# Gram products beside the up and sp products, and off-diagonal products in three pieces, in a fused delta-rule attention and expert-layer kernel

## The chip, the cores and the metric

One core of one Trainium2 chip runs the kernel. Its engines are named as in the profile: PE (TensorE; PEld is its weight load), DVE (VectorE), ACT (ScalarE), POOL (GpSimd) and SP (the queue that issues transfers). The metric is the device time of one execution in microseconds (us); the time of a kernel is the median of its runs.

## The reference

Three stages follow each other, all in float32. For each of 32 (batch, head) pairs a state of 48 by 48 runs through 768 positions:

```python
k_n = k / (np.linalg.norm(k, axis=-1, keepdims=True) + 1e-06)
for t in range(S):
    y[:, :, t] = q_t @ state
    v_old = state.T @ k_t
    state = state + b_t * outer(k_t, v_t - v_old)
```

Its output, as 3072 rows of 384, goes through two expert layers, whose products are the bulk of the arithmetic:

```python
x = (x @ w_a) * (x @ w_b) @ w_out                       # width 1536
h = x @ w_in                                            # width 2048
out = (np.maximum(h, 0) + alpha * np.minimum(h, 0)) @ w_out
```

## The kernel before

**Chunks.** The sequence is cut into NSC = 6 chunks c of 128 positions, and each chunk into two steps j of 64. The recurrence inside a step is solved as a triangular system. The 32 pairs lie as 16 pairs on each of two halves of the 128 partitions (index x), so a product of 48 or 64 rows uses one quarter (a quadrant) of PE's array, and the two halves use two quadrants that share neither rows nor columns.

**Per chunk.** `gram` (L210) computes for four of the 16 pairs the Gram products of the next chunk N: keys with keys and keys with queries, 128 columns wide, in one PSUM bank, and DVE masks them at L222 (keys, into `ef`), L223 and L224 (queries, back into `Z`). Eight such blocks make a chunk's Grams. `fold` (L263) copies a part of `ef` on ACT. `inverting` (L270) then inverts the 32 by 32 diagonal blocks by 30 rounds of two DVE instructions (L293, L294), and `diagonal` (L297) transposes the result into `hw` (L301) and `TT` (L305). `offdiag` (L312) forms the off-diagonal part: for each j first w = ef x hw (L321, copied into `hw` by ACT at L324), then xx = hw x TT (L332, copied into `TT` at L335), all in tiles of 32 by 32. `step` (L339) then runs rp (v minus keys times state, L354, L355), up (L364, copied into `SU`), sp (the next state, L377) and yp (the output, L385, L386), each in two halves of 8 pairs with one bank each.

**Order.** All engines follow the order in which the program is written. The first expert layer of the chunk before is a generator `moe1`: p products (x times w_a or w_b, L578) and o products (L580), one matmul at a time. `run(moe, n, PIECE)` puts n of them between two blocks of the attention, n being FILLS[c] = 10. A counter `now` counts matmuls (plus PIECE for a block); what DVE, ACT and POOL do in the background (weight decoding, the inversion through `leisurely`) is emitted when that counter says that the engine is free. The loop around the change, in c = 1 to 4:

```python
for j in range(2):
    for i, _ in enumerate(A.step(c, j, L)):
        going = run(moe, fill, PIECE) and going
        for _ in range(2):
            if grams:
                A.gram(N, *grams.pop(0), "chain" if c == 1 else "pre")
                going = run(moe, fill, PIECE) and going
```

So two Gram blocks follow each of the first four blocks of step 0. Of PSUM's banks, `chain` has two, `pre` one, `ab` two for the p products, `out` three for o. In c = 1 `pre` belongs to the decoding of weights, and Grams and off-diagonal products use `chain`; later they use `pre`.

**Chunk 0** has no expert products yet. It runs the same functions with `early` in place of `run`, and there the Grams of chunk 1 were made ahead (`gram_keys`, `gram_queries`). Its `offdiag` blocks stand between masks and folds of chunk 1, in the loop over `A.offdiag` with OFF. After chunk 5 the rest of the first and then the second layer run without attention.

Of the kernel before, what the change touches and what calls it, by code (L numbers as in the profile page):

```python
# [31 lines left out]
FILLS = (0, 10, 10, 10, 10, 10)  # L32
# [18 lines left out]
OFF = (6, 6, 10, 10)  # L51
# [29 lines left out]
class Attention:  # L81
# [128 lines left out]
    def gram(s, L, j, i4, tag="pre"):  # L210

        nc = s.nc
        Z, ef = L["Z"][j], L["ef"]
        if j not in L.setdefault("mb", {}):
            s.masks(L, j)
        mb = L["mb"][j]
        g = s.bank("g", tag).rearrange("p (i n) -> p i n", n=128)
        for i in range(4):
            nc.tensor.matmul(g[0:64, i, :], Z[64:112, 0, i4 + i, :], Z[64:112, 0:2, i4 + i, :], start=True, stop=True)  # L219
            nc.tensor.matmul(g[64:128, i, :], Z[0:48, 0, i4 + i, :], Z[0:48, 0:3:2, i4 + i, :], start=True, stop=True)  # L220
        u0 = j * 16 + i4
        nc.vector.tensor_tensor(ef[:, u0 : u0 + 4, :], g[:, :, 0:64], mb[:, i4 : i4 + 4, :], ALU.mult)  # L222
        nc.vector.tensor_tensor(Z[0:64, 1, i4 : i4 + 4, :], g[0:64, :, 64:128], mb[0:64, i4 : i4 + 4, :], ALU.mult)  # L223
        nc.vector.tensor_tensor(Z[64:128, 2, i4 : i4 + 4, :], g[64:128, :, 64:128], mb[64:128, i4 : i4 + 4, :], ALU.mult)  # L224
        s.spend(DVE, 5)

    def gram_keys(s, L, j, i8, tag):

        nc, Z = s.nc, L["Z"][j]
        g = s.bank("g", tag).rearrange("p (i n) -> p i n", n=64)  # L230
        for i in range(8):
            nc.tensor.matmul(g[0:64, i, :], Z[64:112, 0, i8 + i, :], Z[64:112, 0, i8 + i, :], start=True, stop=True)
            nc.tensor.matmul(g[64:128, i, :], Z[0:48, 0, i8 + i, :], Z[0:48, 0, i8 + i, :], start=True, stop=True)
        return g

# [4 lines left out]
    def gram_queries(s, L, j, i8, tag):  # L240

        nc, Z = s.nc, L["Z"][j]
        g = s.bank("gq", tag).rearrange("p (i n) -> p i n", n=64)
        for i in range(8):
            nc.tensor.matmul(g[0:64, i, :], Z[64:112, 0, i8 + i, :], Z[64:112, 1, i8 + i, :], start=True, stop=True)
            nc.tensor.matmul(g[64:128, i, :], Z[0:48, 0, i8 + i, :], Z[0:48, 2, i8 + i, :], start=True, stop=True)
        return g
# [64 lines left out]
    def offdiag(s, L, tags=("pre", "pre")):  # L312
# [3 lines left out]
        for j in range(2):  # L316
            w = s.bank("w", tags[j]).rearrange("p (i n) -> p i n", n=32)
            for i in range(16):
# [3 lines left out]
            for x in range(2):  # L322
                r = slice(64 * x + 32, 64 * x + 64)
                nc.scalar.copy(hw[r, j * 16 : j * 16 + 16, :], w[r])  # L324
                s.spend(ACT, 2.3)
            yield
        for j in range(2):
            xx = s.bank("xx", tags[j]).rearrange("p (i n) -> p i n", n=32)
            for i in range(16):
# [3 lines left out]
            for x in range(2):  # L333
                r = slice(64 * x, 64 * x + 32)
                nc.scalar.copy(TT[r, j * 16 : j * 16 + 16, 32:64], xx[r])  # L335
                s.spend(ACT, 2.3)
            yield

    def step(s, c, j, L):  # L339

        nc, ap = s.nc, s.ap
        st = c * 2 + j
# [5 lines left out]
        for o, hs in halves:  # L348
# [3 lines left out]
            rp = bank("rp")  # L352
            for i in range(8):
                nc.tensor.matmul(rp[0:64, i, :], Z[64:112, 0, o + i, :], SU[0][64:112, o + i, :], start=True, stop=True)  # L354
                nc.tensor.matmul(rp[64:128, i, :], Z[0:48, 0, o + i, :], SU[1][0:48, o + i, :], start=True, stop=True)  # L355
            nc.vector.tensor_tensor(R[:, hs, :], rp, R[:, hs, :], ALU.subtract)
            s.spend(DVE, 2.3)
            yield
        for o, hs in halves:
            up = bank("up")  # L360
            for i in range(8):
                for x in range(2):
                    sl = slice(64 * x, 64 * x + 64)
                    nc.tensor.matmul(up[sl, i, :], s.TT[sl, j, o + i, :], R[sl, o + i, :], start=True, stop=True)  # L364
            for x in range(2):
                sl = slice(64 * x, 64 * x + 64)
                nc.scalar.copy(SU[x][sl, hs, :], up[sl])
                s.spend(ACT, 1.9)
            yield
        for o, hs in halves:  # L370
            if st == 2 * NSC - 1:
                break
            sp = bank("sp")
            for i in range(8):
                for x in range(2):
                    sl = slice(64 * x, 64 * x + 64)
                    nc.tensor.matmul(sp[64 * x : 64 * x + 48, i, :], bk[sl, j, o + i, :], SU[x][sl, o + i, :], start=True, stop=True)  # L377
            nc.vector.tensor_tensor(SN[1][0:48, hs, :], SU[0][64:112, hs, :], sp[0:48], ALU.subtract)
            s.spend(DVE, 4.4)
            nc.vector.tensor_tensor(SN[0][64:112, hs, :], SU[1][0:48, hs, :], sp[64:112], ALU.subtract)  # L380
            yield
# [22 lines left out]
def attn_moe_kernel(tc, kt, qt, kn, vn, beta, w_a, w_b, w_o, w_in, w_o2, alpha, out):  # L404
    nc = tc.nc
    with ExitStack() as ctx:
# [96 lines left out]
        def prepare():  # L503
# [3 lines left out]
            if m is not None:  # L507
                while (m, i) not in decoded or {"u", "g"} & set(under):
# [129 lines left out]
        GRAMS = [(j, i4) for j in range(2) for i4 in range(0, 16, 4)]  # L638
# [42 lines left out]
        def staging():  # L681

            t = None
            for tag, k in STAGES:
                for q in range(k):
                    while under.count(tag) >= RING.get(tag, 1) or tag in closed:
                        yield None
                    under.append(tag)
                    rooms.append(tag)
# [13 lines left out]
        def decode1(depth):  # L703
# [5 lines left out]
            raw = None if W[m][0] is None and m == M1 - 2 and "late" in under else next(words)  # L709
# [84 lines left out]
        for i, _ in enumerate(A.offdiag(L, ("chain", "chain"))):  # L794
            if i in (1, 2):

                for h in range(2):
                    A.mask_keys(N, i - 1, 8 * h, keys.pop(0))
                    spend(DVE, 3)
                A.fold(N, i - 1)  # L800
            if i == 2:
                rooms1.append("pre")
                inv = A.inverting(N, room)
                idle = leisurely(inv)
            early(OFF[i])
        L["y"] = [None, None]
# [25 lines left out]
        for c in range(NSC):  # L832
# [3 lines left out]
            if c > 0:  # L836
                N = A.load(c + 1) if c + 1 < NSC else None
                grams = []
# [14 lines left out]
                for i, _ in enumerate(A.offdiag(L, ("chain", "chain") if c == 1 else ("pre", "pre"))):  # L853
                    going = run(moe, fill, PIECE) and going
                    if N is not None:
                        if i == 1:
                            norms = A.norms(N)
                        if i >= 1:
                            next(norms, None)
                if N is not None:  # L860
                    A.masks(N, 0)
                    grams = list(GRAMS)
                closed.clear()
                L["y"] = [None, None]
                for j in range(2):
                    for i, _ in enumerate(A.step(c, j, L)):
# [4 lines left out]
                        for _ in range(2):  # L871
# [189 lines left out]
```

## Time and profile before

| what | us |
|---|---|
| median of 3 runs | 1169.42 (1168.88 to 1171.29) |
| the profiled execution, its own time | 1172.91 |
| its span, first to last instruction | 1171.2 |
| PE busy | 1085.0 |
| DVE busy | 683.3 |
| POOL busy | 540.9 |
| ACT busy | 463.1 |

The span is that of one profiled execution; 1.7 us lie around it. The busy time of an engine is the union of its instructions' times. A product of two float32 operands shows as two records of PE, so the 16 matmuls of an up block are 32 records. Times in the trace count from the span's start. The five chunks with expert products go from the first w product of one chunk to that of the next.

### The profile page before, as it was taken

The page shows a single profiled execution, that of the slowest core. Times are in us where ns is not written, and L with a number is a line of the kernel's source. Part 1 is how long each engine was busy: PE and PEld are TensorE (multiplying, and loading weights), DVE is VectorE, ACT ScalarE, POOL GpSimd, SP SyncE. Part 2 cuts the span into 40 slices and gives each one's busy share as a digit, 9 for nine tenths or more (in the row PEclk, how much of TensorE's full clock was granted, in tenths as well). Part 3 has the DMA queues.
Part 4 walks back from the last instruction along what each step waited for, and adds up shares of the span by engine and source line. Part 5 has one row for each costly group of instructions (what it writes and reads, how often), then busy time and mean ns, then how long its engine had stood idle before and what let it go on. Part 6 is the DMA issues. An engine that isn't in the chain of part 4 may idle for free.

```text
span 1171.2 us, 22896 instructions
## 1 busy us (share of the span) xinstructions
PE 1085.0 (93%) x9536; PEld 905.4 (77%) x9536; DVE 683.3 (58%) x1141; ACT 463.1 (40%) x895; POOL 540.9 (46%) x459
## 2 busy tenths in 40 slices
PE   5367999699998999999999999999999999999998
PEld 5365677477776777777777887789999999999997
DVE  7887679843894389438927558834343433434332
ACT  4364664353335333533367577622221112112111
POOL 6264686434443444545436668823333333333332
PEclk9577999889999999999999999999999999999999
DMA  9105232300030003000023134010201002020101
GB/s 279 61 30 150 95 110 82 95 29 15 2 96 29 15 2 96 29 15 4 12 69 110 55 104 154 26 55 1 54 1 42 14 1 55 1 55 1 27 1 27
DMA packets 25591, 61.35 MB, mean 52 GB/s; under 512 B 4496, under 2 KB 7568, under 8 KB 25488
## 3 DMA queue, kind: packets, MB, share of 16 engines
q1 hardware_dynamic: 25168, 59.50, 17.2%
q8 instruction: 75, 1.23, 0.4%
q10 hardware_dynamic: 320, 0.39, 0.1%
q14 instruction: 28, 0.23, 0.1%
HBM read 50.44 MB, written 9.44 MB: 51 GB/s over the span
## 4 chain that ended last, share of the span: by engine, by line
PE 57%; DVE 19%; issue 3%; ACT 3%; POOL 1%; DMA 0%; ACTq 0%; DVEq 0%; POOLq 0%
PE h L489 17%; PE o L942 17%; PE p L578 11%; PE o L580 6%; DVE itmp L293 5%; DVE eu L294 5%; PE g L219 2%; DVE a L533 2%; DVE wu L477 1%; DVE v L763 1%; ACT wu L476 1%; PE up L364 1%; PE xx L332 1%; PE rp L354 1%; DVE hw L301 1%
## 5 line engine op out<-in xcount | busy, mean ns | idle before, releaser
L578 PE MATMUL p<-x,wu 128*128 128x512 f32 x1296 | 345.8, 408 | 18.5 <-DVE a L533 9.5
L578 PEld LDWEIGHTS p<-x,wu 128*128 128x128 f32 x1296 | 240.9, 192 | 78.1 <-issue 8.2
L477 POOL TENSOR_TENSOR wu<-W,wu 128x384 fp32r<-128x384 f32 x166 | 175.4, 1060 | 238.0 <-ACT wu L476 208.3
L477 POOL TENSOR_TENSOR g<-neg,g 128x512 fp32r<-128x512 f32 x95 | 123.3, 1298 | 276.7 <-ACT g L476 276.7
L942 PE MATMUL o<-v,g 128*128 128x384 f32 x1152 | 217.8, 337 | 0.2 <-ACT g L476 0.2
L489 PE MATMUL h<-x,v 128*128 128x512 f32 x864 | 215.2, 393 | 0.0
L942 PEld LDWEIGHTS o<-v,g 128*128 128x128 f32 x1152 | 204.7, 188 | 9.1 <-ACT g L476 0.5
L933 DVE TENSOR_SCALAR neg<-h,al 128x512 f32<-128x512 f32 (+1 forms) x97 | 72.3, 746 | 218.2 <-PE h L489 217.3
L476 ACT CAST g<-neg 128x512 fp32r<-128x512 f32 (+1 forms) x97 | 59.7, 615 | 325.5 <-DVE neg L934 311.9
L489 PEld LDWEIGHTS h<-x,v 128*128 128x128 f32 x864 | 160.7, 188 | 29.3
L580 PE MATMUL o<-g,wu 128*128 128x512 f32 x648 | 173.8, 402 | 0.8 <-DVE wu L477 0.5
L580 PEld LDWEIGHTS o<-g,wu 128*128 128x128 f32 x648 | 119.5, 190 | 29.7 <-issue 2.9
L476 ACT CAST wu<-W 128x384 fp32r<-128x384 f32 x216 | 107.7, 510 | 23.8 <-PE o L580 12.4
L542 POOL TENSOR_TENSOR g<-a,g 128x512 fp32r<-128x512 f32 x71 | 94.4, 1329 | 40.0 <-ACT g L537 40.0
L537 ACT CAST g<-a 128x512 fp32r<-128x512 f32 x72 | 44.5, 618 | 126.1 <-DVE a L533 125.8
L533 DVE TENSOR_TENSOR a<-p,a 128x512 f32<-128x512 f32 x72 | 49.5, 687 | 67.1 <-PE p L578 40.6
L477 DVE TENSOR_TENSOR wu<-W,wu 128x384 fp32r<-128x384 f32 x50 | 49.9, 998 | 58.5 <-ACT wu L476 57.2
L293 DVE TENSOR_TENSOR itmp<-eu 128x30 f32<-128x30 f32 (+14 forms) x120 | 68.2, 568 | 3.2
L294 DVE TENSOR_TENSOR eu<-eu,itmp 128x30 f32<-128x30 f32 (+14 forms) x120 | 67.5, 563 | 4.1
L934 DVE SCALAR_TENSOR_TENSOR neg<-h,neg 128x512 f32<-128x512 f32 (+1 forms) x97 | 66.5, 686 | 3.3
L530 ACT COPY a<-p 128x512 f32<-128x512 f32 x72 | 42.0, 584 | 45.8 <-PE p L578 34.0
L321 PE MATMUL w<-hw,ef 32*32 32x32 f32 x768 | 17.3, 207 | 28.7 <-DVE hw L301 24.0
(111 smaller groups left out, 1308.8 us busy)
## 6 DMA issues: line engine op xcount, KB each, us to landing
v<-in_w_in_dram SPq DMA_DIRECT2D x16, 384.0 KB, 3.5
v<-in_w_o_dram SPq DMA_DIRECT2D x16, 384.0 KB, 3.3
k<-in_kn_dram SPq DMA_DIRECT2D x6, 768.0 KB, 6.6
Z<-in_kt_dram SPq DMA_DIRECT2D x24, 192.0 KB, 7.2
Z<-in_qt_dram SPq DMA_DIRECT2D x24, 192.0 KB, 6.6
v<-in_vn_dram SPq DMA_DIRECT2D x12, 384.0 KB, 3.1
raw<-in_w_a_dram SPq DMA_DIRECT2D x12, 384.0 KB, 6.2
raw<-in_w_b_dram SPq DMA_DIRECT2D x12, 384.0 KB, 5.0
```

The costliest lines, as they stand in the source:

```text
L293: nc.vector.tensor_tensor(tm, a, b, ALU.mult)
L294: nc.vector.tensor_tensor(eu[:, m + 1 : 32, 0:m], eu[:, m + 1 : 32, 0:m], tm, ALU.add)
L476: nc.scalar.copy(dst[:, 0], src)
L477: eng.tensor_tensor(dst[:, 1], src, f32(dst[:, 0]), ALU.subtract)
L489: nc.tensor.matmul(p, u[:, a, kk * 128 : kk * 128 + 128], xs[kk][:, b], start=(n == 0), stop=(n == 3 * KT - 1))
L533: nc.vector.tensor_tensor(a[m], ab.pop((m, 1)), a[m], ALU.mult)
L542: (nc.vector if last else nc.gpsimd).tensor_tensor(g[m][:, 1], a[m], f32(g[m][:, 0]), ALU.subtract)
L578: nc.tensor.matmul(ab[m, t], wu, X[c][kk][:, q], start=(n == 0), stop=(n == 8))
L580: nc.tensor.matmul(o[kk], wu, g[m][:, q], start=(m == 0 and n < 3), stop=(m == M1 - 1 and n > 5),)
L933: nc.vector.tensor_scalar(t[:, cs], h[:, cs], 0.0, al[:, m : m + 1], ALU.min, ALU.mult)
L934: nc.vector.scalar_tensor_tensor(t[:, cs], h[:, cs], 0.0, t[:, cs], ALU.max, ALU.add)
L942: nc.tensor.matmul(o[n], g[:, a, n * 128 : n * 128 + 128], V[m][1][:, b], start=(m == 0 and i == 0), stop=(m == M2 - 1 and i == 2),)
```

## The change

1. `gram` goes. Its products are cut into blocks of eight pairs and 64 columns, keys or queries alone (`grams`), and become mates: `mate` hands `step` a function that issues the two Gram products of pair i, and `step` calls it right after the two products of its own pair i. up and sp have mates, in step 0 the four blocks of keys, in step 1 the four of queries. A mate uses the two quadrants that its host doesn't, and a bank of its own: `chain` in c = 1 and `pre` later.
2. `offdiag` makes three pieces of four: w of j=0; xx of j=0 with w of j=1, pair by pair; xx of j=1, which is returned as a function and is the mate of the first rp of step 0, two pairs for one of rp. In chunk 0 the third piece stands by itself.
3. The mask tiles of the two steps get a room each (`mk`, `mb`), and both are made after the second rp. The stages of `norms` move from between the off-diagonal pieces to the first rp blocks.
4. There are fewer stops, so the fill between them is 13 in c = 1 and 14 later, and OFF has three entries. Rooms of staged weights are now told apart by number and not by tag alone.

```diff
-FILLS = (0, 10, 10, 10, 10, 10)
+FILLS = (0, 13, 14, 14, 14, 14)
-OFF = (6, 6, 10, 10)
+OFF = (8, 10, 12)
@@ masks
-            mb = s.ap.tile([128, 16, 64], F32, tag="mb", name="mb", bufs=1)
+            mb = s.ap.tile([128, 16, 64], F32, tag=("mk", "mb")[j], name="mb", bufs=1)
@@ gram goes; new
+    def grams(s, L, j, i8, tag, a, b, go=True):
+        nc, Z = s.nc, L["Z"][j]
+        g = s.bank("g", tag).rearrange("p (i n) -> p i n", n=64)
+        def products(i):
+            nc.tensor.matmul(g[0:64, i, :], Z[64:112, 0, i8 + i, :], Z[64:112, a, i8 + i, :], start=True, stop=True)
+            nc.tensor.matmul(g[64:128, i, :], Z[0:48, 0, i8 + i, :], Z[0:48, b, i8 + i, :], start=True, stop=True)
+        if not go:
+            return g, products
...
+    def mate(s, L, j, i8, tag, queries, then=None):
+        def begun():
+            g, products = s.grams(L, j, i8, tag, *((1, 2) if queries else (0, 0)), go=False)
+            def keep():
+                if queries:
+                    s.mask_queries(L, j, i8, g, s.nc.vector)
+                else:
+                    s.mask_keys(L, j, i8, g)
...
+            return products, keep
+        return begun
@@ offdiag, its last lines (first and second issue w and xx of one j)
+        products, keep = first(0, "chain")
+        for i in range(16):
+            products(i)
+        keep()
+        yield
+        a, b = second(0, "chain"), first(1, tag)
+        for i in range(16):
+            a[0](i)
+            b[0](i)
+        b[1]()
+        a[1]()
+        def last():
+            products, keep = second(1, tag)
+            return lambda i: (products(2 * i), products(2 * i + 1)), keep
+        yield last
@@ step, at rp, up and sp alike
+            beside, keep = mate()
             for i in range(8):
...
+                beside(i)
...
+            keep()
@@ chunk 0
-            if i in (1, 2):
-                for h in range(2):
-                    A.mask_keys(N, i - 1, 8 * h, keys.pop(0))
+            for h in range(2):
+                A.mask_keys(N, i, 8 * h, keys.pop(0))
@@ chunks 1 to 5
+                mates = [[last, None], [None, None]]
...
+                    for q in range(2):
+                        mates[q] += [A.mate(N, *jg, tag, q == 1, after.get(jg) if q == 0 else None) for jg in HALF]
...
+                    for i, _ in enumerate(A.step(c, j, L, mates[j])):
+                        if N is not None and j == 0 and i < 2:
+                            next(norms, None)
+                            if i == 1:
+                                A.masks(N, 0)
+                                A.masks(N, 1)
                         going = run(moe, fill, PIECE) and going
```

Three places show it in the order of instructions. A row gives the line, the operation, the output and inputs and the output's shape; xN is the number of equal instructions in a row.

PE before, in step 0 of c = 3: an up block by itself, nine and one expert products, and the start of a Gram block (each L219 with an L220, four times).

```order
L578 MATMUL p<-x,wu 128x512 x9
L364 MATMUL up<-v,TT 64x48 x16
L578 MATMUL p<-x,wu 128x512 x9
L580 MATMUL o_4010<-g,wu 128x512
L219 MATMUL g<-Z 64x128
L220 MATMUL g<-Z 64x128
```

PE in the change, the same up block (its line numbers are those of the changed kernel).

```order
L637 MATMUL p<-x,wu 128x512 x13
L639 MATMUL o_4172<-g,wu 128x512
L418 MATMUL up<-v,TT 64x48 x2
L220 MATMUL g<-Z 64x64
L221 MATMUL g<-Z 64x64
L418 MATMUL up<-v,TT 64x48 x2
```

The 16 up products now come two at a time, with two Gram products of half the width behind each two; no Gram block stands by itself.

PE in the change, the start of the first rp block of the same step, which stood alone before, as the xx block of j=1 did.

```order
L637 MATMUL p<-x,wu 128x512 x14
L405 MATMUL rp<-SU,Z 64x48
L406 MATMUL rp<-SU,Z 64x48
L350 MATMUL xx<-TT,hw 32x32 x4
L405 MATMUL rp<-SU,Z 64x48
L406 MATMUL rp<-SU,Z 64x48
```

Four small xx products now follow each two of rp, eight times.

ACT in chunk 0, before: all four copies of hw, then folds (`ef`) and copies of `TT` in turn.

```order
L324 COPY hw<-w 32x512 x4
L267 COPY ef_183<-ef_183 32x16x32 x2
L335 COPY TT<-xx 32x16x32 x2
L267 COPY ef_183<-ef_183 32x16x32 x2
L335 COPY TT<-xx 32x16x32 x2
```

ACT in chunk 0 in the change.

```order
L339 COPY hw<-w 32x512 x2
L273 COPY ef_183<-ef_183 32x16x32 x2
L339 COPY hw<-w 32x512 x2
L355 COPY TT<-xx 32x16x32 x2
L273 COPY ef_183<-ef_183 32x16x32 x2
L355 COPY TT<-xx 32x16x32 x2
```

The second two copies of hw moved behind the first fold.

## Rows read from the trace of the kernel before

**Rows 1.** The page's first part: busy us, share of the span, instructions.

```profile
PE 1085.0 (93%) x9536; PEld 905.4 (77%) x9536; DVE 683.3 (58%) x1141; ACT 463.1 (40%) x895; POOL 540.9 (46%) x459
```

**Rows 2.** Chunks c=1 to 4: us; busy PE, PEld, DVE, ACT, POOL; clock, DMA share, GB/s.

```profile
108.86:235.68 126.82, 109.57 (x1210) 83.62 (x1211) 100.43 (x179) 67.45 (x135) 79.33 (x72) 0.96 0.29 91
235.68:353.15 117.47, 113.67 (x1232) 88.71 (x1233) 74.06 (x133) 49.57 (x94) 54.72 (x46) 0.97 0.13 35
353.15:469.11 115.96, 112.00 (x1232) 87.45 (x1232) 74.25 (x132) 49.14 (x94) 52.07 (x44) 0.99 0.14 36
469.11:584.07 114.96, 111.99 (x1233) 87.36 (x1232) 73.86 (x132) 49.57 (x95) 54.43 (x47) 0.99 0.05 15
```

**Rows 3.** PE in order of time (start, us, instruction): a Gram block; expert products alone.

```profile
382.80 2.56 PE L578 MATMUL p<-x,wu 128*128 128x512 f32 x10
385.30 0.32 PE L219 MATMUL g<-Z 48*64 48x128 f32 x1
...
386.32 0.74 PE L578 MATMUL p<-x,wu 128*128 128x512 f32 x2
...
667.31 4.24 PE L578 MATMUL p<-x,wu 128*128 128x512 f32 x18
671.39 2.20 PE L580 MATMUL o<-g,wu 128*128 128x512 f32 x9
```

**Rows 4.** PE in order of time: an xx, an up and a sp block, and what follows.

```profile
363.82 1.20 PE L332 MATMUL xx<-TT,hw 32*32 32x32 f32 x64
364.95 2.11 PE L578 MATMUL p<-x,wu 128*128 128x512 f32 x8
...
392.36 1.13 PE L364 MATMUL up<-v,TT 64*64 64x48 f32 x32
393.42 2.34 PE L578 MATMUL p<-x,wu 128*128 128x512 f32 x9
...
413.60 0.92 PE L377 MATMUL sp<-SU,k 64*48 64x48 f32 x32
414.45 0.97 PE L578 MATMUL p<-x,wu 128*128 128x512 f32 x3
```

**Rows 5.** Chunk 0: one stretch's busy times and clock, then PE within it.

```profile
57.30:60.70 3.40, 3.40 (x90) 3.40 (x87) 1.68 (x2) 3.34 (x7) 0.00 (x0) 0.50 0.03 7
...
57.23 0.31 PE L245 MATMUL gq<-Z 48*64 48x64 f32 x1
...
57.24 0.34 PE L364 MATMUL up<-v,TT 64*64 64x48 f32 x2
57.33 0.31 PE L245 MATMUL gq<-Z 48*64 48x64 f32 x1
...
57.35 0.34 PE L364 MATMUL up<-v,TT 64*64 64x48 f32 x2
```

**Rows 6.** Chunk 0, PE at the full clock: Gram products of queries, then yp.

```profile
67.59 0.22 PE L246 MATMUL gq<-Z 48*64 48x64 f32 x1
...
67.88 0.22 PE L246 MATMUL gq<-Z 48*64 48x64 f32 x1
68.03 0.26 PE L385 MATMUL yp<-SU,Z 112*64 112x48 f32 x1
```

**Rows 7.** What PE waited for from 235.68 to 600: total us, times, longest.

```profile
PE w L321 <- DVE hw L301: 6.5, 2, 4.8
```

**Rows 8.** ACT in chunk 0, in order of time: the two folds.

```profile
53.19 1.24 ACT L267 COPY ef<-ef 32x512 f32<-32x512 f32 x2 [2.46 <-DVE ef L238]
...
55.66 1.24 ACT L267 COPY ef<-ef 32x512 f32<-32x512 f32 x2
```

**Rows 9.** After a Gram block of c=1: PE, then DVE; last, c=3's masks by line.

```profile
128.30 0.50 PE L578 MATMUL p<-x,wu 128*128 128x512 f32 x1
...
134.71 0.43 DVE L224 TENSOR_TENSOR Z<-g,mb 64x256 f32<-64x256 f32 x1
...
L222 DVE TENSOR_TENSOR ef<-g,mb 128x256 f32<-128x256 f32 x8 | 3.4, 424 | 14.7 <-PE g L220 10.9 <-POOL mb L202 3.8
```

More of the change, by code (lines that the diff above doesn't have):

```diff
@@ L240, in gram_queries @@
     def gram_queries(s, L, j, i8, tag):
[L242 to L247, printed above, removed]
+        return s.grams(L, j, i8, tag, 1, 2)
     def keep_queries(s, L, j, i8, g):
@@ L321, in offdiag, with keep, second, products @@
                     nc.tensor.matmul(w[64 * x + 32 : 64 * x + 64, i, :], ef[r, j * 16 + i, 32:64], hw[r, j * 16 + i, :], start=True, stop=True)
[L322 to L329, printed above, removed]
+            def keep():
+                for x in range(2):
+                    r = slice(64 * x + 32, 64 * x + 64)
+                    nc.scalar.copy(hw[r, j * 16 : j * 16 + 16, :], w[r])
+                    s.spend(ACT, 2.3)
+            return products, keep
+        def second(j, tag):
+            xx = s.bank("xx", tag).rearrange("p (i n) -> p i n", n=32)
+            def products(i):
                 for x in range(2):
@@ L360, in step @@
             up = bank("up")
+            beside, keep = mate()
             for i in range(8):
@@ L368, in step @@
                 s.spend(ACT, 1.9)
+            keep()
             yield
@@ L373, in step @@
             sp = bank("sp")
+            beside, keep = mate()
             for i in range(8):
@@ L380, in step @@
             nc.vector.tensor_tensor(SN[0][64:112, hs, :], SU[1][0:48, hs, :], sp[64:112], ALU.subtract)
+            keep()
             yield
@@ L507, in prepare @@
             if m is not None:
-                while (m, i) not in decoded or {"u", "g"} & set(under):
+                while (m, i) not in decoded or {"u", "g"} & {u[0] for u in under}:
                     now += 1
@@ L708, in decode1 @@
             m, i = left[0]
-            raw = None if W[m][0] is None and m == M1 - 2 and "late" in under else next(words)
+            raw = None if W[m][0] is None and m == M1 - 2 and any(u[0] == "late" for u in under) else next(words)
             if raw is None:
@@ L793, in attn_moe_kernel @@
         spend(POOL, 8)
-        for i, _ in enumerate(A.offdiag(L, ("chain", "chain"))):
-            if i in (1, 2):
-                for h in range(2):
-                    A.mask_keys(N, i - 1, 8 * h, keys.pop(0))
[L799 to L804, printed above, removed]
-            early(OFF[i])
+        for i, last in enumerate(A.offdiag(L, "chain")):
+            for h in range(2):
+                A.mask_keys(N, i, 8 * h, keys.pop(0))
+                spend(DVE, 3)
+            A.fold(N, i)
+            early(OFF[i])
+        rooms1.append("pre")
+        products, kept = last()
+        for i in range(8):
+            products(i)
+        kept()
+        inv = A.inverting(N, room)
+        idle = leisurely(inv)
+        early(OFF[2])
         L["y"] = [None, None]
```

96 lines of the change are left out of this document (42 added, 54 removed).

## The prediction

> **What bounds the kernel now.** I read the busy line of the page first, then the busy time by chunk, then TensorE in order of time. TensorE is busy 93% of the span [rows 1]. By chunk it is busy 113.67 of 117.47, 112.00 of 115.96 and 111.99 of 114.96 us for c=2, 3 and 4, while VectorE (DVE) has 74 us of work in each of them [rows 2]: in these three chunks TensorE sets the time, and what leaves its queue leaves the clock. Chunk c=1 is different: TensorE 109.57 and DVE 100.43 of 126.82 us. There DVE also decodes weights, and a shorter TensorE queue may meet DVE.
>
> A mixture product of the expert layer (p or o) costs 4.08/18 = 0.227 us: the block of 18 starts at 667.31 and the next at 671.39 [rows 3]. A Gram block is dearer than its products. Ten p before it last from 382.80 to 385.30, 2.50 where ten cost 2.27, and the Gram block runs from 385.30 to 386.32. So 1.02 us for the block and 0.23 for entering and leaving the small tiles: 1.25 us [rows 3]. The reader should see the second number: it is paid for each block, however short.
>
> **The change part by part.** *Gram blocks.* Eight in each of the chunks c=1 to 4 go: 32 x 1.25 = 40.0 us off TensorE. Their products come back as 64 columns, beside the products of up and sp, sixteen pairs of records for each of eight blocks of a chunk. An up block takes 1.06 us (392.36 to 393.42), a sp block 0.85 (413.60 to 414.45) [rows 4]. What a mate adds depends on whether four quadrants really work at once. The trace has one such moment, at granted clock 0.50, the lower level (1.2 GHz): up products and Gram products of queries overlap for some pairs. The Gram pairs start at 57.23 and 57.33, the up pairs at 57.24 and 57.35: each stream holds its own pace of 0.107 us, and neither pays for the other [rows 5]. At the full level a Gram pair takes 0.058 us (67.59 to 67.88 is five) [rows 6], about as much as a pair of up, so the mate should vanish behind it. The upper bound for overlapped work is the densest stretch seen, 64 records of xx in 1.13 us or 17.7 ns each (363.82 to 364.95) [rows 4]: 64 records are then 1.13 us. I take this bound, since the density of four streams at the full level is not in the trace: up +0.07, sp +0.28, 4 x 0.35 = 1.4 a chunk, **5.6 us** in four chunks. The lower bound is up +0 and sp +0.2, 3.2 us; without any overlap each block pays 16 x 0.057 = 0.91, which is 29 us.
>
> A page's rule speaks against it: the Trainium skill, "TensorE: Matmul & The Clock Gate", section Back-to-back issue gap, has a floor of about 25 ns from start to start. As an estimate by it, 64 records would take 1.6 us, and the mates 4 x (0.54 + 0.75) = 5.2 us a chunk instead of 1.4. The 17.7 ns of the xx block [rows 4] is below that floor, so I don't use it.
>
> *Off-diagonal products.* Before, four blocks of 64 records in each of c=1 to 5 cost 1.13 + 0.23 = 1.36 each, 5.44 a chunk [rows 3, 4]. After, the first stays (1.36). The second holds two of the old ones: 1.36 if four small tiles overlap as above, 128 x 17.7 ns + 0.23 = 2.50 if not; I take 1.6, nearer to the overlap of rows 5. The third stands beside rp, whose pairs are paced like those of up: at least +0.1, and at the densest seen 96 x 17.7 ns = 1.70 against 1.06, +0.64; I take 0.3. So 5.44 - 3.26 = 2.2 a chunk, **10.9 us** in five (bounds 4.7 and 13.1).
>
> *DVE.* Three masks of 256 columns a Gram block become one or two of 512 a mated block, about the same sum. Both mask products now stand together on POOL after the second rp, where four blocks go by before the first of j=1 is needed: nothing. The inversion of the next chunk starts after six stretches of 14 products and not after twelve of 10, so it ends earlier against TensorE. TensorE waited 6.5 us for the transposed inverse at the starts of c=2 and 3 [rows 7]; I expect 4 of these back.
>
> *New waits.* In the stage before c=1, ScalarE's second pair of copies of hw now stands behind the fold. The fold waited for DVE until 53.19 and took 1.24 [rows 8]; the second product, the second fold (at 55.66 before) and with it the inversion move by those 1.24 us: +1.2. A mated block in c=1 takes both banks of the chain, which single blocks took in turn before, and both must be free again 13 products later, about 3.2 us; in c=2 to 4 the Gram bank is a single other one, as before, and has 14 products, 3.4 us. In c=1 DVE is late: a Gram block ended at 128.30, and its last mask at 134.71 + 0.43, 6.8 us later [rows 9]. A wait of up to 3.6 us in some of its eight blocks is likely, but it falls on a queue that was waiting for the inverse anyway; I charge 2. In c=3 DVE stood waiting for Gram products (10.9 us) [rows 9], so nothing there.
>
> *Sum.* -40.0 + 5.6 - 10.9 = -45.3 on TensorE; waits -4 + 1.2 + 2 = -0.8. Total **-46.1**. The profiled execution took 1172.91 (span 1171.2), so 1126.8 there; the median of the runs shown, 1169.42, lies 3.5 lower, and the same sum gives **1123.3 us**. After c=5 the program is the same, and its stages keep their time.
>
> **Rivals.** (1) *Tile sizes don't mix.* rp uses 64 by 64 tiles, xx 32 by 32. Where the trace changes from Gram tiles of 64 rows to the yp products of 128 rows, the streams do not overlap, and 0.15 us pass from start to start (67.88 to 68.03) in place of 0.058 [rows 6]. If every change in the mixed block costs this, its eight rounds take 8 x (0.058 + 0.15 + 3 x 0.035 + 0.15) = 3.7 us, +2.6 against rp alone; that is 2.3 more than I charged, five times: 1134.8. Against it: those two also claim the same rows and columns of the array, which rp and xx do not. The Trainium skill, "TensorEngine Tiling (Array Packing)", section Key Properties, says that changing the tiling mode drains the engine; by this rule the rival would hold, and no run here shows the two sizes side by side.
>
> (2) *The mates do not overlap* at the full level, and the change only saves entering and leaving: 29 in place of 5.6 and the off-diagonal gain cut to its lower bound 4.7 gives 1123.3 + 23.5 + 6.2 = 1153. For it: the overlap in rows 5 is short and at half clock. Against it: nothing there slows down at all.
>
> (3) *Chunk c=1 belongs to DVE.* Its share of the gain, 10.0 - 1.4 + 2.2 = 10.8 us, is then waited away: 1134. For it the 100.43 us of DVE; against it 26 us in which DVE is idle [rows 2].
>
> (4) *Slower: the mask holds the bank.* Each mated block needs the bank that the block before it filled, and DVE empties it in its own order behind the inversion. With the lag of rows 9 (6.8 us) less 3.4, every one of 32 blocks would wait 3.4 us: +109, 1232. It decides the sign from 46.1/32 = 1.4 us a block, that is a lag of 4.8 us from the last product to the last mask, in all chunks. Against it: in c=2 to 4 DVE was early, not late.
>
> **How the numbers follow.** Forecast 0.52, (1) 0.20, (2) 0.12, (3) 0.09, (4) 0.04; 0.03 is left for no visible effect. The forecast's own bounds: 40.0 - 3.2 + 13.1 and 6 of waits reach down to 1113; with a boundary of c=1 that closes wholly, 1107. Upward, 40.0 - 5.6 - 4.7 without any wait recovered gives 1143, and both (1) and (3) together 1146. (2) and (4) and no effect, 0.19, stay out. Range **1107 to 1148**. A difference of 0.2% is about what the runs can tell from none. Faster 0.93 (all but the last two), same 0.03, slower 0.04.
>
> **What would show it.** Right: records of up and g start in turn, and the mated blocks take about 1.1 us; rp with xx takes 1.3 to 1.4; c=2 to 4 last some 104 us from w to w, c=1 some 115; the wait for hw shrinks. Rival 1 shows as a rp block near 3.7 us, rival 2 as mated blocks near 2 us, rival 3 as c=1 above 122 us, rival 4 as waits of g or up for DVE's masks. The forecast is wrong if c=2 to 4 stay above 110 us.

## The result and the profile after

The changed kernel takes **1158.68 us** (median of 4 runs, 1155.48 to 1160.27) against 1170.36 for the kernel before in the same comparison (1168.88 to 1172.73): ratio 0.9895, 95% interval 0.9866 to 0.9924. It is 1% faster, by 12 us where 46 were forecast, and lies outside the range. The profiled execution has a span of 1158.5 us and is the longest of the four. By chunk, from one w block to the next (the prologue up to the first):

| stretch | before | after | change | forecast |
|---|---|---|---|---|
| prologue, to w of c=1 | 108.9 | 110.1 | +1.2 | +1.2 |
| c=1 | 126.8 | 138.1 | +11.3 | -11.8 |
| c=2 | 117.5 | 107.4 | -10.1 | -13.5 |
| c=3 | 116.0 | 107.5 | -8.5 | -12.0 |
| c=4 | 115.0 | 108.0 | -7.0 | -11.0 |
| c=5 to the end | 587.1 | 587.4 | +0.3 | -2.2 |

The forecast column takes the "some 115" and "some 104" of the prediction, which is why it adds up to a little more than its 46.1. The first row below is the page's busy line, answering to [rows 1].

```profile
PE 1063.0 (92%) x10048; PEld 896.3 (77%) x10048; DVE 682.8 (59%) x1092; ACT 463.5 (40%) x895; POOL 546.4 (47%) x460
```

PE lost 22 us of busy time, but the span only 12.7. The next rows, busy time by stretch as in [rows 2], say where: first the chunks c=1 to 4, then three short stretches, namely the products behind the block that holds rp and xx in c=2, that block itself in c=3, and the products behind it in c=5.

```profile
110.09:248.23 138.14, 111.13 (x1339) 85.86 (x1339) 105.48 (x167) 68.31 (x135) 80.25 (x71) 0.91 0.28 81
248.23:355.63 107.40, 104.94 (x1361) 84.08 (x1361) 71.72 (x121) 49.47 (x94) 54.25 (x45) 0.97 0.14 39
355.63:463.11 107.48, 104.01 (x1361) 83.17 (x1361) 74.62 (x120) 49.38 (x95) 55.90 (x46) 0.98 0.14 39
463.11:571.08 107.97, 103.71 (x1361) 83.13 (x1360) 71.67 (x119) 49.54 (x95) 55.47 (x47) 0.98 0.05 16
...
262.93:265.30 2.37, 2.37 (x10) 1.89 (x7) 1.98 (x2) 1.51 (x4) 0.00 (x0) 0.50 0.00 0
366.50:370.44 3.94, 3.94 (x97) 3.17 (x97) 1.28 (x3) 2.50 (x4) 0.00 (x0) 1.00 0.02 7
584.51:587.50 2.99, 2.99 (x11) 2.41 (x8) 0.33 (x1) 2.19 (x4) 0.53 (x1) 0.50 0.56 171
```

In c=2 to 4 PE still sets the time (104 of 107 us busy). In c=1 it stands 27 us, and what it does there takes 111.13 us although the Gram blocks are gone (109.57 with them, [rows 2]): the granted clock is 0.91 in place of 0.96, and the block of rp and xx is dear. The rp block of c=3 lasts 3.94 us where 1.3 to 1.4 was forecast, and behind it, in c=2 and c=5, PE ran for a while at 0.50, the lower of its two levels (1.2 GHz).

PE in order of time (start, us, instruction) in c=3 shows the block from inside, and then the beginning of a mated block of up and g:

```profile
366.51 0.25 PE L405 MATMUL rp<-SU,Z 48*64 48x48 f32 x1
...
366.60 0.22 PE L405 MATMUL rp<-SU,Z 48*64 48x48 f32 x1
366.61 0.22 PE L406 MATMUL rp<-SU,Z 48*64 48x48 f32 x1
366.76 0.31 PE L350 MATMUL xx<-TT,hw 32*32 32x32 f32 x8
367.00 0.25 PE L405 MATMUL rp<-SU,Z 48*64 48x48 f32 x1
...
382.91 0.23 PE L418 MATMUL up<-v,TT 64*64 64x48 f32 x2
382.94 0.22 PE L220 MATMUL g<-Z 48*64 48x64 f32 x1
382.95 0.22 PE L221 MATMUL g<-Z 48*64 48x64 f32 x1
382.97 0.22 PE L418 MATMUL up<-v,TT 64*64 64x48 f32 x2
383.00 0.22 PE L220 MATMUL g<-Z 48*64 48x64 f32 x1
```

The mates do what the forecast expected: an up pair every 0.06 us with a Gram pair in between, the whole block 1.09 us (382.82 to 383.91) against 1.06 for up alone. The rp and xx records do not mix like this: a round of four rp and eight xx takes 0.49 us (366.51 to 367.00), and from rp to xx (366.61 to 366.76) 0.15 us pass.

What PE waited for in c=1 (engine, line, released by: total us, times, longest), and below the same for c=2 to 4:

```profile
PE g L220 <- DVE v L408: 5.2, 1, 5.2
PE w L334 <- DVE hw L307: 4.4, 2, 3.8
PE g L220 <- DVE Z L266: 3.0, 2, 1.8
...
PE g L220 <- DVE Z L266: 5.0, 4, 1.9
PE g L220 <- issue: 3.9, 2, 2.3
PE w L334 <- DVE hw L307: 3.8, 1, 3.8
```

In c=1 nearly all of the 27 us are waits on DVE and ACT, 5.2 us at most. In c=2 to 4 a Gram block of queries waits now and then for the mask of the one before (Z at L266); the 3.9 us put to "issue" stand before such blocks too. The 3.8 us for hw is one wait that both views show: it ends at 248.23, the start of c=2. The boundary waits that answer to [rows 7] are so down from 6.5 to 3.8 us.

### The profile page after: what moved, and what is told of

It reads as the page before. It is cut to its first block, busy times and chain, and to the rows that moved or that the text cites. A ratio compares the mean times of both kernels' runs of the same rounds, so it can differ in the third digit from the quotient of the medians.

```text
span 1158.5 us, 23809 instructions
## 1 busy us (share of the span) xinstructions
PE 1063.0 (92%) x10048; PEld 896.3 (77%) x10048; DVE 682.8 (59%) x1092; ACT 463.5 (40%) x895; POOL 546.4 (47%) x460
## 4 chain that ended last, share of the span: by engine, by line
PE 66%; DVE 19%; ACT 6%; issue 5%; POOL 3%; DMA 1%; ACTq 0%; POOLq 0%; DVEq 0%
PE h L548 17%; PE o L1007 17%; PE p L637 15%; PE o L639 8%; DVE itmp L299 4%; DVE eu L300 2%; DVE wu L536 2%; PE rp L405 2%; DVE inv L300 1%; PE xx L350 1%; PE yp L444 1%; DVE v L824 1%; DVE Z L266 1%; DVE a L592 1%; ACT wu L535 1%
## 5 line engine op out<-in xcount | busy, mean ns | idle before, releaser
L637 PE MATMUL p<-x,wu 128*128 128x512 f32 x1296 | 337.3, 407 | 8.5 <-DVE a L592 3.8
L637 PEld LDWEIGHTS p<-x,wu 128*128 128x128 f32 x1296 | 246.5, 194 | 64.5 <-ACT a L589 4.3
L536 POOL TENSOR_TENSOR wu<-W,wu 128x384 fp32r<-128x384 f32 x167 | 178.0, 1069 | 216.9 <-ACT wu L535 204.5
L639 PE MATMUL o<-g,wu 128*128 128x512 f32 x648 | 179.6, 414 | 2.5 <-ACT wu L535 0.6
L639 PEld LDWEIGHTS o<-g,wu 128*128 128x128 f32 x648 | 125.0, 199 | 32.4 <-ACT wu L535 1.5
L535 ACT CAST wu<-W 128x384 fp32r<-128x384 f32 x216 | 108.1, 511 | 36.2 <-POOL W L507 14.5
L220 PE MATMUL g<-Z 48*64 48x64 f32 x768 | 62.6, 243 | 29.9 <-DVE Z L266 8.0
L220 PEld LDWEIGHTS g<-Z 48*64 48x64 f32 x768 | 56.7, 155 | 31.5 <-issue 12.6
```

Source lines behind the costliest of these rows:

```text
L535: nc.scalar.copy(dst[:, 0], src)
L536: eng.tensor_tensor(dst[:, 1], src, f32(dst[:, 0]), ALU.subtract)
L637: nc.tensor.matmul(ab[m, t], wu, X[c][kk][:, q], start=(n == 0), stop=(n == 8))
L639: nc.tensor.matmul(o[kk], wu, g[m][:, q], start=(m == 0 and n < 3), stop=(m == M1 - 1 and n > 5),)
```

## The experiments

Medians, ratios to the kernel before with their 95% interval, and the length of c=1 and c=2 in the profiled execution. e12 to e15 leave out part of the weight decoding: they show where time goes and are no versions of the kernel.

| run | us | ratio | c=1 | c=2 |
|---|---|---|---|---|
| before | 1170.4 | | 126.8 | 117.5 |
| the change | 1158.7 | 0.9895 (0.9866 to 0.9924) | 138.1 | 107.4 |
| e1_last_alone | 1146.3 | 0.9786 (0.9765 to 0.9807) | 132.8 | 108.1 |
| e2_rp_then_xx | 1143.4 | 0.9761 (0.9746 to 0.9776) | 135.2 | 104.2 |
| e3_late_inversion | 1208.0 | 1.0312 (1.0290 to 1.0334) | 138.3 | 122.2 |
| e4_c1_old_grams | 1149.9 | 0.9822 (0.9803 to 0.9840) | 130.8 | 107.7 |
| e5_xx_behind_c1_old | 1135.9 | 0.9704 (0.9689 to 0.9718) | 127.0 | 105.4 |
| e6_c1_inversion_mid | 1142.2 | 0.9757 (0.9740 to 0.9775) | 135.0 | 105.2 |
| e7_offdiag_only | 1178.0 | 1.0051 (1.0031 to 1.0070) | 127.5 | 119.0 |
| e8_four_rounds | 1149.4 | 0.9825 (0.9808 to 0.9842) | 135.9 | 106.4 |
| e9_c1_stretch16 | 1145.2 | 0.9786 (0.9766 to 0.9807) | 135.5 | 105.0 |
| e10_c1_stretch10 | 1138.2 | 0.9721 (0.9702 to 0.9739) | 131.0 | 104.1 |
| e11_c1_keys_first | 1139.4 | 0.9732 (0.9710 to 0.9755) | 128.5 | 105.1 |
| e12_thin_decode_mates | 1125.8 | 0.9614 (0.9579 to 0.9650) | 118.3 | 105.2 |
| e13_thin_decode_alone | 1124.3 | 0.9602 (0.9566 to 0.9638) | 115.9 | 105.5 |
| e14_thinner_decode_mates | 1115.0 | 0.9526 (0.9468 to 0.9584) | 107.3 | 104.1 |
| e15_thinner_decode_alone | 1121.0 | 0.9577 (0.9531 to 0.9623) | 113.8 | 104.5 |

### The block of rp and xx

**e1_last_alone**, the third piece as a block of its own:

```diff
-                mates = [[last, None], [None, None]]
+                products, kept = last()
+                for i in range(8):
+                    products(i)
+                kept()
+                going = run(moe, fill, PIECE) and going
+                mates = [[None, None], [None, None]]
```

> The third off-diagonal piece no longer stands beside rp: it is a block of its own, with a stretch of products behind it, in chunks c=1 to 5; everything else as in the changed kernel. Theory A (the two tile sizes do not mix): the block of 3.93 us becomes rp 1.06 and xx 1.13 plus 0.23 for entering, 1.5 us less in each of five chunks, and the clock's drop to 0.50 that followed it in c=1, 2 and 5 (1.4, 1.4 and 2.7 us) is gone too: 1158.7 - 7.5 - 5.5 = about 1146. Theory B (the missing gain lies in waits for DVE and its order alone): rp and xx together cost nothing that matters, and the time stays within 3 us of 1158.7. Theory C (the mixed block also holds DVE's queue up in c=1, where DVE stood 7.6 us waiting for that rp): as A, and c=1 falls from 138.1 below 131, total below 1142.

1146.3, as theory A says; B falls. c=1 is 132.8, not below 131, so C's stronger claim falls too.

**e2_rp_then_xx**, the same records in the same block, but xx behind rp:

```diff
                 nc.tensor.matmul(rp[64:128, i, :], ...)
+            for i in range(8):
                 beside(i)
```

> The third piece stays in the rp block, but all 32 rp records come first and all 64 xx records behind them, one change of tile size in place of fifteen. Theory A (each change of size costs about 0.1 us more than the pace): 1.06 + 0.15 + 1.1 = 2.3 us a block in place of 3.93, 1.6 x 5 = 8 us less and the clock's drop of 5.5 gone: about 1145. Rival (it is the third stream of work as such that is dear, 96 records at whatever order): the block stays near 3.9 us and the time at 1158.7.

The windows of e2: c=1, c=2, c=4, and in c=2 the rp and xx block and the 14 products behind it.

```profile
109.59:244.83 135.24, 109.14 (x1339) 84.60 (x1340) 106.21 (x167) 68.02 (x135) 80.30 (x71) 0.91 0.29 83
244.83:349.02 104.19, 101.78 (x1363) 81.89 (x1365) 71.99 (x121) 49.30 (x94) 54.57 (x45) 0.98 0.15 40
...
453.43:558.14 104.71, 102.04 (x1365) 82.01 (x1366) 72.83 (x120) 49.27 (x95) 55.70 (x47) 0.98 0.05 17
...
255.51:257.70 2.19, 2.19 (x97) 2.10 (x96) 0.82 (x2) 2.14 (x5) 0.37 (x1) 1.00 0.23 84
257.70:261.10 3.40, 3.40 (x20) 2.55 (x15) 2.08 (x2) 2.61 (x5) 0.64 (x1) 1.00 0.02 5
```

2.19 us for the block and 3.40 for the products behind it: what made it 3.93 was the order, not the records, and with it goes the stretch at half clock behind the block. Nothing overlaps even so: 2.19 is 1.06 for rp and 1.13 for xx. 15.3 us come back, of which 5 x 1.74 = 8.7 are the block itself and 5.6 the products behind it in c=1, 2 and 5. In c=3 and c=4 the two profiles differ by a further 1.3 and 1.5 us, in waits for Z and the clock behind them; that the order of the block does this too is not shown. c=2 to 4 are now 104.2, 104.4 and 104.7 us, the 104 of the forecast.

**e8_four_rounds**, to price one change of size:

```diff
-                beside(i)
+                if i % 2 == 1:
+                    for q in range(i - 1, i + 1):
+                        beside(q)
```

> As the changed kernel, but the mixed block alternates in four rounds (four rp records pairwise, then sixteen xx) in place of eight: 7 changes of tile size where there were 15, and 1 in e2. If every change costs the same, (3.93 - 2.20)/14 = 0.124 us, the block takes 2.20 + 6 x 0.124 = 2.94 us, and the time is near 1143.4 + 5 x 0.74 = 1147 with the clock kept, up to 1152 if it still drops behind the block. If the price is of the first changes alone, the block stays above 3.5.

In the windows of e8, the block in c=3 and the products behind it:

```profile
362.00:364.94 2.94, 2.94 (x97) 2.56 (x96) 1.02 (x2) 2.89 (x5) 0.00 (x0) 1.00 0.26 97
364.94:369.94 5.00, 5.00 (x20) 3.72 (x14) 2.26 (x3) 2.97 (x7) 1.42 (x2) 0.66 0.02 5
```

2.94 us, as worked out: 15, 7 and 1 changes give 3.93, 2.94 and 2.20, **0.124 us a change**. The Trainium skill, "TensorEngine Tiling (Array Packing)", section Key Properties, says that changing the tiling mode drains the engine; these three blocks agree. With seven changes the clock still fell once, here in c=3. Over all kept profiles, one execution each, the products behind the block ran below the full clock in 13 of 20 cases with 15 changes (the change, e3, e4, e7), in 1 of 5 with 7, and in none of 50 with one (e2, e5, e6, e9 to e15).

**e7_offdiag_only**, Grams as before in all chunks, stretches of 10, off-diagonal products as in the change (the `gram` of the kernel before goes back in, and its calls):

```diff
-FILLS = (0, 13, 14, 14, 14, 14)
+FILLS = (0, 10, 10, 10, 10, 10)
...
                 if N is not None:
+                    finish(norms)
+                    A.masks(N, 0)
+                    grams = [(q, i4) for q in range(2) for i4 in range(0, 16, 4)]
+                elif False:
```

> The off-diagonal part of the change alone: Grams in all chunks as before (32 blocks of their own, stretches of 10), off-diagonal products in the three pieces of the change. From the parts read in the changed kernel's trace: 1.36 + 1.45 + 2.87 = 5.68 us a chunk in place of 5.44, five times +1.2, the lower clock behind the mixed blocks up to +5, the prologue's +1.2, less up to 4 of waits for hw: 1168 to 1177, no gain from this part, against the 10.9 that were forecast for it (1159).

1178.0, 1 us above the range expected: alone, the off-diagonal part makes the kernel slower by 0.5% (0.3 to 0.7), where the forecast had a gain of 10.9 us. Its mixed blocks took 3.93 to 4.43 us. The windows of e7, the block in c=2 and the ten products behind it:

```profile
247.32:251.61 4.29, 4.29 (x97) 3.44 (x97) 1.56 (x1) 2.67 (x4) 1.00 (x1) 0.87 0.35 127
251.61:256.18 4.57, 4.57 (x15) 3.15 (x11) 3.17 (x11) 2.38 (x5) 1.93 (x2) 0.50 0.00 0
```

In four of the five chunks these ten products took 4.07 to 4.57 us in place of 2.50, 7.8 us together where up to 5 was expected.

### The query masks

**e3_late_inversion**, the inversion begun behind the last query mate:

```diff
                     inv = A.inverting(N)
-                    background.append(leisurely(inv))
+                    if not (c > 0):
+                        background.append(leisurely(inv))
...
                         going = run(moe, fill, PIECE) and going
+                        if N is not None and j == 1 and i == 5 and (c > 0):
+                            background.append(leisurely(inv))
```

> The inversion of the next chunk starts only behind the last query mate (second sp block of j=1), in c=1 to 4, and not behind the last key mate. Theory D (the query masks wait on DVE behind the inversion and hold the bank): the long mated blocks of j=1 in c=2, 3, 4 (2.9, 4.4 and 6.7 us over 1.09 and 3.40) go back to 1.09, 14 us less; the inversion then ends late at the chunk's end and w waits for hw, up to 6 us in each of four chunks. So 1145 to 1158, with the waits moved from g to w. Rival (the late masks come from other DVE work: products of a, weights): the blocks stay long and the hw wait comes on top: 1165 or more. In c=1 the wait of 5.2 us of up for DVE's v goes if the inversion was in front of it, and stays if decoding was.

Half right: every mated block of c=2 is back at 1.09 us, and up's wait for v in c=1 is gone (its next block waits 4.0 us for ACT's copy of `SU` instead), so both came from the inversion ahead in DVE's queue. But the price at the end was badly misjudged, and the time, 1208.0, lies far above theory D's 1145 to 1158. PE's waits in e3:

```profile
PE w L334 <- DVE hw L307: 75.8, 6, 15.6
```

14.1 to 15.2 us at the end of each of c=1 to 4 (the 15.6 lies in the prologue, where the changed kernel waits too): the some 3 us a chunk before the blocks of queries, (5.0 + 3.9)/3, are the cheaper place for the same DVE work.

### What holds c=1

**e4_c1_old_grams**, c=1 alone as before (the edit of e7 with `if c == 1`, so with stretches of 10 there):

> Chunk c=1 alone forms its Grams as before (eight blocks of their own with 128 columns, stretches of 10 products, masks of 256 columns); off-diagonal products and chunks 2 to 4 as in the changed kernel. Theory E (in c=1 the mates are what costs: both chain banks at once, and DVE's masks and the earlier inversion late): c=1 takes 126.8 - 2.2 + 2.9 + 1.4 = about 129 in place of 138.1, total about 1149. Theory C (the mixed rp block ahead of it throws c=1 out of step, whatever the Grams do): c=1 stays at 135 or more and the total within 3 us of 1158.7.

c=1 is 130.8 and the time 1149.9: theory E, and C falls for good. Which part of the edit does it, the mates or the longer stretches that came with them, is a question for e10. **e5_xx_behind_c1_old** joins e2 and e4:

> Both corrections together: xx behind rp with one change of tile size (as in e2), and c=1 with its Grams as before (as in e4). If the two causes are separate, c=1 goes from 130.8 (e4) to about 126.4 (its mixed block 4.53 to 2.2, the run behind it 4.56 at the lower clock to 2.5), that is 8.8 less than the 135.2 of e2: 1143.4 - 8.8 = about 1134.6. If they are one cause (the mixed block throwing c=1 out of step), e4's gain is gone in it and the time stays at 1141 to 1145.

The window of c=1 in e5:

```profile
109.62:236.60 126.98, 108.72 (x1211) 83.38 (x1211) 101.52 (x179) 68.15 (x135) 79.97 (x71) 0.96 0.30 88
```

1135.9: the two causes add up, and this is the best version measured that does all the work, 35 us below the kernel before. Note what c=1 is here: 126.98 us, with Gram blocks as before and a little less off-diagonal work it takes as long as before (126.82 in [rows 2]); with mates and stretches of 13 (e2), and some 9 us less for PE to do (8 x 1.25 less 4 x 0.27), it takes 8 us longer. Eight runs look for the reason.

**e6_c1_inversion_mid** (the edit of e3 in c=1 only and at `i == 1`, on e2):

> As e2, but in c=1 alone the next chunk's inversion starts later, behind the second rp block of j=1, in place of behind the last key mate. Theory F (in c=1 the inversion ahead in DVE's queue is what makes rp's result and the query masks late): the waits for v (5.2 us), Z (1.5) and SU (1.5) of j=1 go, xp starts some 8 us earlier, and DVE's busy time in c=1 falls from 106 towards 100 where it runs less beside POOL; the wait for hw at the end grows from 3.8 to 6 to 11. Total 1138 to 1145. Rival G (both chain banks taken by up and its mate): the waits of j=1 stay, now on decoding, and only the end grows: 1147 or more.

```profile
109.93:244.97 135.04, 106.47 (x1338) 82.33 (x1339) 96.39 (x167) 68.05 (x135) 79.87 (x71) 0.89 0.27 83
```

The wait for v goes and DVE's busy time falls by 10 us (106.21 to 96.39, the window above), yet c=1 is as long as in e2: the next block of up now waits 3.6 us for ACT's copy of `SU`, and the wait for hw at the end grew from 3.8 to 10.3. xp, the transposes of the chunk's output near its end, started 3 us earlier, not 8. Waits move, the sum stays.

**e9_c1_stretch16** and **e10_c1_stretch10** (FILLS[1] = 16 and 10, on e2):

> As e2, with stretches of 16 products in place of 13 between the blocks of c=1. Theory H (a mated block takes both chain banks that the block before it filled, and 13 products are too short a time to empty them): with 16 the reuse comes 0.7 us later at each of 19 blocks, the waits of sp, up and g in c=1 shrink, and c=1 goes from 135.2 to 130 or less; total near 1138. Theory I (the banks are not it: the chunk's decoding, on DVE, ScalarE and GpSimd in turn, sets its length, and the mated blocks leave less time for it between two blocks): the waits only move, c=1 stays within 3 us of 135.2, total 1140 to 1146.

> As e2, with stretches of 10 in c=1. Theory H: each reuse comes 0.7 us sooner, waits grow by up to 0.7 at eight mated blocks and at the blocks of j=1, c=1 goes to 138 to 145, the products left over stand at its end: total 1146 or more. Theory I: c=1 stays within 3 us of 135.2; a longer end run gives the inversion cover, so even a gain of up to 3 is possible.

135.5 and 131.0. Theory H expected 130 or less and then 138 or more; it fails both times, the second with the sign reversed, so the time to empty the banks is not what holds c=1. Theory I is right on e9, and 1 us off its bound on e10, which gained 4 us with the mates in place.

**e11_c1_keys_first** (e5, but the Gram blocks of c=1 hold the products of one kind, keys first):

> As e5 (xx behind rp, c=1 without mates), but the Gram blocks of c=1 hold 64 columns and all key blocks come first, so that the inversion starts as early as in the mated version, four stretches (14 us) before e5's. If the early inversion is what costs c=1 its 8 us, c=1 returns to about 135 and the total to 1143. If the mating is (its banks, or the time that it takes from the other engines), c=1 stays at 127 or below, because the wait for hw at its end (6.7 in e5) shrinks by up to 6 us: total 1130 to 1136.

128.5, between the two, but nearer to e5: keys first and the early inversion cost c=1 1.5 us. The windows of c=1, e10 and then e11:

```profile
109.74:240.74 131.00, 107.78 (x1339) 82.53 (x1339) 103.51 (x168) 67.98 (x135) 78.77 (x70) 0.92 0.28 86
```

```profile
109.79:238.32 128.53, 111.10 (x1338) 85.48 (x1339) 108.04 (x167) 68.05 (x135) 79.75 (x71) 0.96 0.30 87
```

The mating can't be priced against e2 alone, for e5 and e11 have stretches of 10 there and e2 has 13. With the same 10, e10 has mates and is 2.5 us longer in c=1 than e11 and 4.0 longer than e5. So of the 8 us, 4.2 go with the longer stretches (e2 to e10), 2.5 with the mating and 1.5 with the early inversion, in one execution each. The medians of e10 and e11, 1138.2 and 1139.4, don't show the 2.5.

**e12_thin_decode_mates, e13_thin_decode_alone** (on e2 and e5):

```diff
-            nc.vector.tensor_scalar(t, e, 3, ...)
-            nc.vector.scalar_tensor_tensor(t, e, -(2**31), t, ...)
+            w8 = slice(0, 8) if thin[0] else slice(0, DM)
+            nc.vector.tensor_scalar(t[:, w8], e[:, w8], 3, ...)
+            nc.vector.scalar_tensor_tensor(t[:, w8], e[:, w8], -(2**31), t[:, w8], ...)
...
-            nc.gpsimd.tensor_tensor(r, r, t, ALU.add)
+            nc.gpsimd.tensor_tensor(r, r, r if thin[0] else t, ALU.add)
```

> As e2 (mates in c=1, xx behind rp), but for the weights decoded in c=1 VectorE's two steps cover 8 of 384 columns and GpSimd adds a tile to itself: this work is left out, order and waits are kept. VectorE loses 25 x 1.0 us in c=1. Theory I (decoding on VectorE's queue holds c=1): c=1 falls from 135.2 to 112 or less, and lies below that of e13 by most of the 10 us of TensorE work that mates save. Rival J (the mated blocks' own chain of bank, mask and copies holds c=1): c=1 stays above 125 and above e13's.

> As e5 (c=1 with its Grams in blocks of their own), with the same VectorE work of the decoding in c=1 left out. Theory I: c=1 falls from 127.0 to the length of a later chunk with such Grams, 113 to 118. Rival J: it falls likewise, and e12 doesn't follow.

c=1 falls by 17 us with mates and by 11 without. e13 is as expected; for e12 neither theory has the size, and the mated version is still behind. One thing was not kept: POOL's add no longer reads DVE's result and so doesn't wait for it. 22 of its 25 adds have a wait ahead of them in e2, 2 in e12, and an add takes 0.84 us in place of 1.02. What ACT waited for in c=1 of e12:

```profile
ACT wu L538 <- POOL W L510: 12.6, 8, 3.3
ACT g L599 <- DVE a L595: 11.3, 4, 5.2
ACT e L503 <- DVE raw L507: 10.0, 6, 3.2
```

ACT stands in the first row for POOL's add of a decoded weight. One of these waits (3.3 us, to 135.09) stands ahead of the copy of up for which PE's sp then waits 3.0 us. So **e14_thinner_decode_mates** and **e15_thinner_decode_alone** cut that add and ACT's second activation to 8 columns too:

> As e12, and in addition GpSimd's add and ScalarE's second activation of each weight decoded in c=1 cover 8 of 384 columns (this work too is left out; order and waits are kept). Theory I' (the decoding's rounds through ScalarE, VectorE and GpSimd, with the attention's copies queued behind them, are what holds c=1): c=1 falls from e12's 118.3 to 104 to 112, below e15 by 4 or more, as TensorE's saving then shows. Rival J' (the mated blocks' own chain): c=1 stays at 116 or more.

> As e13 (c=1 with Gram blocks of their own), with the same further work left out. Both theories: c=1 stays near e13's 115.9, between 112 and 117, since TensorE's own work and the late inverse set it there.

The windows of c=1, e14 and then e15:

```profile
108.18:215.44 107.26, 97.59 (x1338) 77.34 (x1339) 78.82 (x167) 59.46 (x135) 59.23 (x70) 0.98 0.33 101
```

```profile
108.10:221.90 113.80, 104.04 (x1212) 81.53 (x1213) 73.04 (x179) 59.92 (x135) 58.85 (x70) 0.99 0.31 95
```

Both expectations hold. With little decoding, the mated chunk is 6.5 us shorter than the one with Gram blocks, in line with the 6.45 us of PE's busy time between them. (PE's idle time is alike, 9.7 and 9.8 us, but not its cause: in e15 6.4 us of it are the wait for hw at the end.) So the mates' gain is there, and in c=1 the decoding hides it: its rounds through ACT, DVE, POOL and ACT again, in queues where the attention's copies and masks stand behind it. Why with full decoding the mated version is slower by 8 us, and not equal, isn't settled beyond the parts under e11: the lower clock between waits (0.91 against 0.96) is in it, but no run separates this.

## Why the prediction was wrong

**Right.** *Gram blocks*: they went at the price used; 14 products with the entry take 3.40 us in place of 10 in 2.50, and in c=4 of e2 PE is busy 102.04 us in place of 111.99 [rows 2]. *Mates*: charged up +0.07 and sp +0.28, measured 1.09 for both, +0.03 and +0.24 (64 records at 17 ns each): four quadrants work at once. *The second piece*: 1.6 taken, 1.22 + 0.23 measured. *The prologue*: the second fold starts 3.64 us behind the first (57.09 and 53.45) in place of 2.47 [rows 8], the +1.2 charged; that the whole prologue grew by 1.2 too is partly luck, for with the same code it ends between 107.8 and 110.5 in the other runs. *The boundaries*: 4 us expected back, 2.7 came (6.5 to 3.8). *c=2 to 4*: 104 us, reached by e2 with the mates as they are; that they stood at 107 to 108 is in the main the next point.

**Wrong: "The third stands beside rp ... I take 0.3."** That step took the overlap of rows 5, between tiles of one size, for tiles of two sizes. Measured is 3.93 us against 1.06, so +2.87. Even in the better order of e2 it is +1.13, above the step's upper bound of +0.64: the sizes take turns and do not overlap. The rival that *tile sizes don't mix* held, nearly at its price (3.7); what was said against it, that rp and xx claim other rows and columns, did not help. What neither had is the clock: behind three of the five mixed blocks (c=1, 2 and 5) it was lower for a while, and the next 13 or 14 products took 4.75, 4.80 and 6.06 us in place of 3.18, 3.40 and 3.40, 5.6 us together. In e2, with one change of size, both are gone, and 15.3 us with them.

**Wrong: c=1 "some 115", with "I charge 2" for its waits.** The step that failed is this charge: PE's idle time in c=1 rose from 17.3 us [rows 2] to 27.0, and its own work didn't get shorter. The rival that *c=1 belongs to DVE* was right that the gain there is waited away: with stretches of 10, c=1 takes 131.0 us with mates (e10) and 127.0 with Gram blocks (e5), for some 9 us less work. e12 to e15 show whose it is: the decoding's. 11 us go with DVE's two steps and POOL's wait for them (e5 to e13), and with mates another 11 with the rest of POOL's add and of ACT's second step (e12 to e14). Its argument against, 26 us of idle DVE, misread idle time in a queue that waits in order: DVE's idle time in c=1 of e6 is 39 us, and the chunk is as long. What no case had is a loss of 11 us on top of the missing gain; mates and their longer stretches account for 8 (e5 against e2), about half of it the stretches (e10), and the mixed block and the clock behind it for 3 (e2 against the change).

The two together, 15.3 in all chunks and the 20 us by which c=1 of e2 stands above 115, are the 35 us between 1123.3 and 1158.7. *The mask holds the bank* held in small: 5.0 us of waits for Z in c=2 to 4 and 3.9 more before the same blocks, which go with them in e3. PE's idle time in c=2 to 4 is 10.2 us, and was 10.7 [rows 2], so these waits took what the boundaries gave back.

## What to carry to other kernels

Here products of small tiles in the same tile size and other quadrants ran side by side almost for nothing (32 more records beside up +0.03 us, beside the shorter sp +0.24); between two sizes every change cost, so put them in one group each, not in turns. Before moving work off the engine that is busiest on average, ask stage by stage whose queue ends last: where weights are decoded through three engines in order, less work for TensorE gave no time, and longer stretches between the attention's blocks cost some. When comparing two versions of a stage, keep the other settings alike: half of what looked like the price of the mates was the length of the stretches. A saving that a stage hides showed up once the hiding work was cut to a stub, which told more than moving its waits about.

## What the runs showed of the hardware

A change of tile size between 64 and 32 costs 0.124 us, and a block with 15 such changes, busy 100% by the profile, was followed by the lower clock in 13 of 20 cases; with a single change in none of 50. Four streams on four quadrants run 64 records in 1.09 us.

DVE's steps of the inversion, which have two inputs in SBUF, take 0.41 us for some 240 columns while POOL stands or where they start just ahead of an add of POOL, and 1.36 where the add started first, as in this stretch of the changed kernel (DVE and POOL in order of time; in brackets the idle time before):

```profile
523.64 0.41 DVE L300 TENSOR_TENSOR eu<-eu,itmp 128x238 f32<-128x238 f32 x1
...
524.44 1.00 POOL L536 TENSOR_TENSOR wu<-W,wu 128x384 fp32r<-128x384 f32 x1 [4.49 <-ACT wu L535]
...
525.38 0.41 DVE L299 TENSOR_TENSOR itmp<-eu 128x240 f32<-128x240 f32 x1
...
525.39 1.53 POOL L601 TENSOR_TENSOR g<-a,g 128x512 fp32r<-128x512 f32 x1
525.82 1.36 DVE L300 TENSOR_TENSOR eu<-eu,itmp 128x240 f32<-128x240 f32 x1
```

The step of DVE that starts at 525.82 ends at 527.18, just behind POOL's add (526.92). Of the 240 such steps behind the prologue, of all sizes, the 79 that began while POOL was at work take 1.08 us on average, the 27 in which POOL began later 0.33, and the other 134 0.33. The Trainium skill, "SBUF — State Buffer", section SBUF: two separate sides, says that a DVE operation with two inputs in SBUF and a GpSimd operation that reads SBUF need the same pair of ports, which the one that starts first holds for its whole instruction while the other blocks; the rows agree. In e6, with the inversion further from the decoding, its 60 steps in c=1 take 32.1 us of DVE in place of 42.1 in e2.
